# Attention and mixture-of-experts kernel: both heads of the 64-row query tile on one set of partitions

## The chip, the cores and the metric

The kernel runs on one core of a Trainium2 chip. The metric is the device time of one execution in microseconds (us). Engines go by the names of the profile: PE (matmul), PEld (its weight load), DVE, ACT, POOL, and SP, which issues most transfers.

## What is computed

The reference, cut to what matters (B, H, S, D = 4, 8, 576, 64; 512 columns in the model, 2048 in the hidden layer):

```python
scores = scale * np.matmul(q, k.transpose(0, 1, 3, 2))
a = np.exp(scores - scores.max(-1, keepdims=True))      # causal
a /= a.sum(-1, keepdims=True) + 1e-09
local = np.matmul(a, v)
phi = lambda x: np.where(x > 0, x, np.exp(x) - 1.0) + 1.0
mem_out = (phi(q) @ M_prev) / (phi(q) @ z_prev + 1e-6)
g = 1.0 / (1.0 + np.exp(-beta))
x = (g * mem_out + (1 - g) * local)                     # to [2304, 512]
r = np.maximum(x @ w_in, 0.0)
out = (s * (r * r) + b) @ w_out
```

## The kernel before, in words

There are three stages. The first runs from the start to about 271 us: the attention of 16 pairs of heads, four batches of four pairs, g = 0 to 15, with the first product (x @ w_in) of the batches that are done woven in. The second, to 357 us, is the rest of the first product, while `w_out` is converted (`conv64`). The third is the second product (`product`).

**A pair.** The two heads j = 0, 1 lie on partitions 0 to 63 and 64 to 127 of the operands of PE. The 576 query rows are cut into tiles i = 0 (64 rows) and 1 to 4 (128 rows each). `scores` (L357) works in three steps, named here Sg.0 (tiles 3 and 0), Sg.1 (tiles 2 and 1) and Sg.2 (tile 4, which takes both of the `sb` buffers). Pairs below 8 multiply in float32 (L370), the others ("fast") in three products of a float32r high and low part (L364), which `split` (L391) makes. For each tile and head `red` (L374, DVE) adds the mask and takes the smallest of each row, `ex` (L381, ACT) takes the exponential and its row sum, DVE sums and inverts (L440, L441), and `scale` (L386, POOL or DVE) scales. Tile 0 uses all 128 partitions for each head in this, with its 64 rows there twice. `phi` (L284) puts phi(q)/(phi(q)·z) of each tile beside it in `P` (`put`, L316). `bank` (L459) transposes `P` in four steps Tg.0 to Tg.3. Each of them reads two halves of the partitions, which go to two `tb` buffers: partitions 0 to 63 (half h0) and 64 to 127 (h1). The step Tg.3 holds the first-column blocks of tiles 0, 1 and 2, and tile 0 is read from h1 alone. `copy` (L472, ACT or DVE) takes the buffers to SBUF. `second` (L510, step Ag) multiplies by V and M, and L541 (ACT) and L542 (DVE) write x as a high and a low part, `xs`, with the first 64 rows apart in `x4`.

**The first product.** A group m (m0 to m40) is one block of 128 hidden columns of one batch (`first`, L596). Its PE work is two halves of six matmuls (`mm1`, L581), each half for two pairs. Its result is taken out of PSUM by a `Relu` on ACT (L609) and stored by SP (L610). `HOME` says whether it lies in a `tb` or an `sb` buffer; m40 lies in `sb`. The weights are converted in pieces (`convert`, L550); `HIGH` and `LOW` choose their engine. The second stage goes on with the same `mm1` into eight `hps` tiles, which take the PSUM of all `sb` and `tb` buffers over, the first that of the buffer sb0.

**What sets the order.** In the first stage each step carries the keys that it reads and writes, and a table of numbers, `ORDER`, says for each engine in which order its steps are issued; `Plan.deal` (L76) interleaves them, and puts warm-up matmuls (L247) into gaps of PE. Letters in `RELU`, `ZMUL`, `PUTS`, `COPY`, `SCAL` and `QL` choose the engine of a step for each pair. In the later stages a scheduler orders ACT and DVE.

```python
            for i, c0, n, o in group:                  # scores, L358
                if fast:                               # L359
                        if i == 0 and h == 0:          # bank, L465
                            continue
```

Of the kernel before, what the change touches and what calls it, by code (L numbers as in the profile page):

```python
# [141 lines left out]
def attention_moe_kernel(  # L142
# [187 lines left out]
    def attention(g):  # L330
# [78 lines left out]
        for v, group in enumerate(visits):  # L409
# [3 lines left out]
            if fast:  # L413
                cost = sum(n + 32 for _, _, n, _ in group) / 800 + 0.05
            add("PE", cost, lambda group=group, ps=ps: scores(group, ps), r,
                [(x, u, k) for x in ("qh", "ql") for k in range(2)] if fast else [("qk", u, k) for k in range((1, 2, 2, 3)[v] if g == 0 else 1)] + [("qk", 0, "d")] * (g == 0),
                [("sc", g, v), "visit"], take=[(ps, "S")] * (2 if v == len(visits) - 1 else 1), mode="row")
# [5 lines left out]
            tiles = [(i, o - c0) for i, c0, n, o in group if c0 + n == QW[i]]
            for k, (i, o) in enumerate(tiles):
                for j in range(2):
# [9 lines left out]
            keys = [("sm", u, i, j) for i in mine for j in range(2)]  # L435
            inv = [("sr", u, i, j) for i in mine for j in range(2)]
# [574 lines left out]
```

## Time and profile before

| | |
|---|---|
| runs | 540.35, 540.95 and 540.98 us, median 540.95 us |
| the profiled execution | 540.74 us |
| its span, first to last instruction | 538.9 us (1.84 us lie around it) |
| granted clock of TensorE | 1.00 throughout |
| busy | PE 529.4, DVE 406.8, ACT 408.1, POOL 276.4 us |
| moved by transfers | 81.51 MB |

The busy times are to be read by stage. In the second and third stage the order of PE hardly leaves a gap, and in the first stage the stretch up to some 56 us, before the first group m0, is another case than what follows it.

### The profile page before, as it was taken

The page shows a single profiled execution, that of the slowest core. Times are in us where ns is not written, and L with a number is a line of the kernel's source. Part 1 is how long each engine was busy: PE and PEld are TensorE (multiplying, and loading weights), DVE is VectorE, ACT ScalarE, POOL GpSimd, SP SyncE. Part 2 cuts the span into 40 slices and gives each one's busy share as a digit, 9 for nine tenths or more (in the row PEclk, how much of TensorE's full clock was granted, in tenths as well). Part 3 has the DMA queues.
Part 4 walks back from the last instruction along what each step waited for, and adds up shares of the span by engine and source line. Part 5 has one row for each costly group of instructions (what it writes and reads, how often), then busy time and mean ns, then how long its engine had stood idle before and what let it go on. Part 6 is the DMA issues. An engine that isn't in the chain of part 4 may idle for free.

```text
span 538.9 us, 11602 instructions
## 1 busy us (share of the span) xinstructions
PE 529.4 (98%) x4158; PEld 444.4 (82%) x4158; DVE 406.8 (75%) x986; ACT 408.1 (76%) x898; POOL 276.4 (51%) x275
## 2 busy tenths in 40 slices
PE   8989999999999999999999999999999999999997
PEld 6767777777878778877788888899999998999996
DVE  5999998998877958334169796435798889889873
ACT  6999999889987637547346679769987887897840
POOL 4999557663784623022100001407768768768760
PEclk9999999999999999999999999999999999999999
DMA  7666667755243621121294746356354353452101
GB/s 223 183 178 193 227 219 253 227 155 196 89 150 101 223 84 59 61 79 44 90 376 165 267 174 219 128 192 204 110 161 121 115 167 114 129 174 89 40 30 40
DMA packets 56666, 81.51 MB, mean 151 GB/s; under 512 B 7584, under 2 KB 39072, under 8 KB 56608
## 3 DMA queue, kind: packets, MB, share of 16 engines
q1 hardware_dynamic: 54064, 78.63, 44.8%
q10 hardware_dynamic: 2544, 2.14, 1.2%
q8 instruction: 33, 0.54, 0.4%
q14 instruction: 25, 0.20, 0.1%
HBM read 57.15 MB, written 23.59 MB: 150 GB/s over the span
## 4 chain that ended last, share of the span: by engine, by line
PE 90%; ACT 6%; DVE 2%; issue 1%; DMA 1%; ACTq 0%; DVEq 0%
PE yps L866 12%; PE yps L870 11%; PE sb L520 7%; PE tb L586 7%; PE tb L587 6%; PE tb L588 6%; PE hps L586 5%; PE hps L587 5%; PE hps L588 5%; PE yps L869 5%; PE yps L868 5%; PE tb L468 4%; PE sb L364 4%; ACT P L383 3%; PE sb L370 2%; PE sb L586 1%
## 5 line engine op out<-in xcount | busy, mean ns | idle before, releaser
L389 POOL TENSOR_SCALAR P<-P,sr,omg 128x448 f32<-128x448 f32 (+4 forms) x120 | 89.2, 758 | 37.0 <-DVE sr L441 26.3
L870 PE MATMUL yps<-rb,op 128*128 128x256 f32 x360 | 101.1, 281 | 0.0
L383 ACT ACTIVATE P<-P,mn 128x448 f32<-128x448 f32 (+4 forms) x160 | 90.0, 568 | 9.6 <-DVE mn L377 9.3
L377 DVE CUSTOM_DVE_ANT_0 P<-sb,mask 128x320 f32<-128x320 f32 (+4 forms) x160 | 72.6, 480 | 24.4 <-PE sb L364 21.8
L866 PE MATMUL yps<-rb,op 128*128 128x512 f32 x216 | 76.9, 396 | 0.0
L870 PEld LDWEIGHTS yps<-rb,op 128*128 128x128 f32 x360 | 67.9, 189 | 0.0
L846 POOL TENSOR_TENSOR sum<-src 128x512 f32<-128x512 f32 x10 | 13.0, 1298 | 91.2 <-ACT src L830 76.6
L854 POOL TENSOR_TENSOR op<-src,op 128x512 fp32r<-128x512 f32 x30 | 43.9, 1484 | 20.2 <-ACT op L853 20.1
L877 DVE TENSOR_TENSOR yu<-yu,yps 128x256 f32<-128x256 f32 x90 | 36.5, 414 | 20.0 <-PE yps L870 19.0
L866 PEld LDWEIGHTS yps<-rb,op 128*128 128x128 f32 x216 | 40.6, 188 | 9.0
L468 PEld LDWEIGHTS tb<-ident,P 64*128 64x128 f32 x928 | 35.9, 139 | 9.6 <-issue 4.3
L468 PE MATMUL tb<-ident,P 64*128 64x64 f32 x928 | 40.9, 226 | 2.2 <-DVE xs L542 0.7
L868 PE MATMUL yps<-rb,op 128*128 128x256 f32 x144 | 40.5, 281 | 0.0
L869 PE MATMUL yps<-rb,op 128*128 128x256 f32 x144 | 40.5, 281 | 0.0
L853 ACT CAST op<-src 128x512 fp32r<-128x512 f32 x50 | 30.5, 615 | 12.0 <-PE yps L870 9.6
L854 DVE TENSOR_TENSOR op<-sum,op 128x512 fp32r<-128x512 f32 x36 | 38.7, 1075 | 0.3 <-ACT op L853 0.2
L593 ACT ACTIVATE r<-hps 128x256 f32<-128x256 f32 x62 | 21.8, 385 | 19.4 <-DMA r_d<-r 14.4
L854 POOL TENSOR_TENSOR op<-w1H,op 128x512 fp32r<-128x512 f32 x24 | 35.0, 1489 | 0.0
L318 POOL TENSOR_TENSOR P<-qs,nrm 128x384 f32<-128x384 f32 (+1 forms) x24 | 18.8, 797 | 31.5 <-DVE nrm L311 23.0
L586 PE MATMUL tb<-xs,w0H 128*128 128x512 f32 x80 | 32.9, 412 | 0.0
L383 ACT ACTIVATION_READ_ACCUMULATOR P<-P,mn 128x1 f32 x160 | 32.3, 202 | 0.0
L370 PE MATMUL sb<-qk 64*128 64x288 f32 (+4 forms) x192 | 30.3, 411 | 1.9 <-DVE mn L377 1.7
(177 smaller groups left out, 1618.5 us busy)
## 6 DMA issues: line engine op xcount, KB each, us to landing
r_d<-r SPq DMA_DIRECT2D x41, 256.0 KB, 2.3
src<-r_d SPq DMA_DIRECT2D x20, 512.0 KB, 4.4
qk<-in_qk_t_dram SPq DMA_DIRECT2D x15, 576.0 KB, 5.0
raw<-in_moe_w_out_dram SPq DMA_DIRECT2D x16, 512.0 KB, 6.2
w1H<-r_d SPq DMA_DIRECT2D x16, 512.0 KB, 4.7
xa<-in_moe_w_in_dram SPq DMA_DIRECT2D x12, 512.0 KB, 4.8
r_d<-r SPq DMA_DIRECT2D x48, 128.0 KB, 1.9
qs<-in_q_rows_dram SPq DMA_DIRECT2D x16, 320.0 KB, 3.2
```

Source lines behind the costliest of these rows:

```text
L377: nc.vector.tensor_tensor_reduce(P[:, j, PB[i] + 64:PB[i] + 64 + n], at(ps, j, o, n), m, -SCALE, 3.0e38, ALU.add, ALU.min, mn[:, j, i:i + 1])
L383: nc.scalar.activation(pt, pt, AF.Exp, scale=-1.0, bias=mn[:, j, i:i + 1], accum_out=sm[:, j, i, 0:1])
L389: e.tensor_scalar(pt, pt, sr[:, j, i:i + 1], omg[:, h:h + 1], ALU.mult, ALU.mult)
L468: nc.tensor.transpose(TB[ps[h]][:, o[h]:o[h] + 64], P[rs, j, c:c + 128], ident[rs, rs], tile_position=(64 * h, 0))
L586: nc.tensor.matmul(ps, lhsT=wH[:, p, fs], rhs=xs[:, 0], start=p == 0, stop=False)
L587: nc.tensor.matmul(ps, lhsT=wH[:, p, fs], rhs=xs[:, 1], start=False, stop=False)
L588: nc.tensor.matmul(ps, lhsT=wL[:, p, fs], rhs=xs[:, 0], start=False, stop=p == NP - 1)
L854: (nc.gpsimd if m in ONPOOL else nc.vector).tensor_sub(L, x, H.bitcast(F32))
L866: nc.tensor.matmul(tile, lhsT=H, rhs=B, start=f == 0, stop=False)
L868: nc.tensor.matmul(ps, lhsT=H, rhs=B[:, 0], start=f == 0, stop=False)
L869: nc.tensor.matmul(ps, lhsT=H, rhs=B[:, 1], start=False, stop=False)
L870: nc.tensor.matmul(ps, lhsT=L, rhs=B[:, 0], start=False, stop=f == KF - 1)
```

## The change

1. Tile 0: the rows of head j go to partitions 64j to 64j + 63 of one slot of `P`. `red` works on 64 partitions for each head. One exponential, sum, reciprocal and scale then serve both heads; the exponential waits for both reductions. The scale needs the gates of both heads in one column, `OM`, which POOL fills once at the start. `phi` still leaves phi of tile 0 in a slot of each head, and one added 64 x 64 multiplication writes head 1's on its partitions.
2. Tg.3 transposes tile 0 of head 0 from half h0 and that of head 1 from h1: five transposes in each half, where there were four and six. Its buffers are copied in two pieces each (256 and 64 columns), four copies where there were two.
3. Fast pairs: tile 0's scores are taken in float32 like those of the first eight pairs; the split of q leaves 128 columns out.
4. `EARLY` is 2: m0 and m1 are issued in quarters, one for each pair (six quarters behind A3, the first of both ahead of it).
5. All letters, `HOME` and `ORDER` are new.

```diff
-                if fast:
+                if fast and i:
...
         def red(i, j, o, ps):
             n = QW[i]
+            if i == 0:
+                rs = slice(64 * j, 64 * j + 64)
+                nc.vector.tensor_tensor_reduce(
+                    P[rs, 0, PB[0] + 64:PB[0] + 128], at(ps, j, o, n)[rs], mask[rs, 576:640], -SCALE, 3.0e38, ALU.add, ALU.min, mn[rs, 0, 0:1])
+                return
...
-            e.tensor_scalar(pt, pt, sr[:, j, i:i + 1], omg[:, h:h + 1], ALU.mult, ALU.mult)
+            e.tensor_scalar(pt, pt, sr[:, j, i:i + 1], omg[:, h:h + 1] if i else OM[:, p:p + 1], ALU.mult, ALU.mult)
...
-            for k, (a, z) in enumerate(((QF, QF + S), (0, QF))):
+            for k, (a, z) in enumerate(((QF, QF + S), (128, QF))):
...
-                    add("ACT", EXP[i], lambda i=i, j=j: ex(i, j), r + 0.15 + 0.01 * k, [("mn", u, i, j)],
-                        [("p", u, i, j), ("sm", u, i, j)])
+                    if i or j:
+                        add("ACT", EXP[i], lambda i=i, j=j * (i > 0): ex(i, j), r + 0.15 + 0.01 * k, [("mn", u, i, h) for h in ((j,) if i else range(2))],
+                            [("p", u, i, j), ("sm", u, i, j)] + [("p", u, 0, 0), ("sm", u, 0, 0)] * (i == 0))
...
-                        if i == 0 and h == 0:
+                        rs = slice(64 * h, 64 * h + 64)
+                        if i == 0:
+                            if h == j:
+                                nc.tensor.transpose(
+                                    TB[ps[h]][:, 0:64], P[rs, 0, c:c + 128], ident[rs, rs], tile_position=(64 * h, 0))
                             continue
...
-            elif h:
-                put(F[:, :, 0:384].rearrange("p j (r c) -> p j r c", c=128)[:, :, :, 0:64],
-                    t[:, 0:384].rearrange("p (j r c) -> p j r c", j=2, c=64))
             else:
-                put(half(F[:, :, 64:320]), t[:, 0:256].rearrange("p (j r c) -> p j r c", j=2, c=64))
+                put(half(F[:, :, 64:320]), t[:, 64:320].rearrange("p (j r c) -> p j r c", j=2, c=64))
+                put(F[:, h, 0:64], t[:, 0:64])
...
+        if EARLY:
+            for p in range(NP):
+                add("PE", cost / 2, lambda p=p: mm1(part(), b, f, p, 1), 1000 + m - NP + p,
...
-    HIGH, LOW = "PPAPAAPPAAAAAAAAAAPA", "PDPDDPPDDDPDPDDDDDDD"
+    HIGH, LOW = "AAPPAAPAAAAPAAAAAAPA", "PPPDDDPPDDDDDDDPDDDD"
...
-    EARLY = 1
+    EARLY = 2
```

The table's new order at the places of which the prediction speaks. First PE around A3, the pair that completes the first batch; L468 is T3.3, L370 S5.1, L520 A3 and L586 to L588 group m0. Before:

```order
L468 MATMUL tb_101<-ident,P_121 128x64
L370 MATMUL sb_97<-qk_107 128x320 x2
L370 MATMUL sb_97<-qk_107 128x192 x2
L520 MATMUL tb_99<-F_125,V_123 64x320 x2
L520 MATMUL tb_99<-pt,V_123 64x256 x2
L520 MATMUL tb_99<-F_125,V_123 64x128 x2
L520 MATMUL tb_98<-F_125,V_123 64x256 x2
L520 MATMUL tb_98<-pt,V_123 64x256 x6
L520 MATMUL tb_98<-F_125,V_123 64x128 x2
L586 MATMUL tb_100<-xs,w0H 128x512
L587 MATMUL tb_100<-xs,w0H 128x512
L588 MATMUL tb_100<-xs,w0L 128x512
```

And now, where L484 is T3.3, L534 is A3, and L600 to L602 are m0 (in tb_101) and m1 (in tb_98):

```order
L484 MATMUL tb_99<-ident,P_122 128x64
L600 MATMUL tb_101<-xs,w0H 128x512
L601 MATMUL tb_101<-xs,w0H 128x512
L602 MATMUL tb_101<-xs,w0L 128x512
L600 MATMUL tb_98<-xs,w0H 128x512
L601 MATMUL tb_98<-xs,w0H 128x512
L602 MATMUL tb_98<-xs,w0L 128x512
L534 MATMUL tb_99<-F_126,V_124 64x320 x2
L534 MATMUL tb_99<-pt,V_124 64x256 x2
L534 MATMUL tb_99<-F_126,V_124 64x128 x2
L534 MATMUL tb_100<-F_126,V_124 64x256 x2
L534 MATMUL tb_100<-pt,V_124 64x256 x6
```

S5.1 now lies ahead of T3.3, and the first quarters of m0 and m1 stand between T3.3 and A3.

Second, ACT at the end of the first stage. L479 copies a buffer of T15.1, L609 is a group's relu (r_127<-sb_96 that of m40), L541 writes the x of A15, L196 and L593 belong to the second stage. Before:

```order
L609 ACTIVATE r_128<-tb_100 128x512
L479 COPY F_125<-tb_100 128x2x4x64
L479 COPY F_125<-tb_101 128x2x4x64
L609 ACTIVATE r_127<-sb_96 128x512
L541 CAST x_137<-sb_97 128x64
L541 CAST xs<-sb_97 128x512
L196 ACTIVATE stg<-raw 128x512 x2
```

And now (L493 copies a buffer of T15.1, L555 writes x, L632 is the relu, L607 belongs to the second stage):

```order
L555 CAST x_138<-sb_97 128x64
L493 COPY pt<-tb_98 128x8x64
L493 COPY pt<-tb_100 128x8x64
L555 CAST x_138<-sb_97 128x64
L555 CAST xs<-sb_97 128x512
L632 ACTIVATE r_128<-sb_96 128x512
L607 ACTIVATE r<-hps 128x256 x2
```

The relu of m40, from sb_96, has moved behind both of A15's casts. On PE, A15 is followed in both kernels by the first matmul into `hps`, which takes that buffer.

Third, DVE at the same end, from the last pair's other tiles on. L377 is a reduction of `red` (128x576 that of S15.2), L389 a scale, L440 and L441 the sum and the inverse, L542 the low part of x for A14. Before:

```order
L389 TENSOR_SCALAR P_121<-P_121,sr_119,omg 128x64 x2
L377 ISA P_121,mn_115<-sb_97,mask 128x576
L377 ISA mn_115 128x1
L389 TENSOR_SCALAR P_121<-P_121,sr_119,omg 128x320 x2
L377 ISA P_121,mn_115<-sb_96,mask 128x576
L377 ISA mn_115 128x1
L440 TENSOR_REDUCE sr_119<-sm_117 128x2
L441 RECIPROCAL sr_119<-sr_119 128x2
L542 TENSOR_TENSOR x_137<-sb_96,x_137 128x64
```

And now (L495 copies a buffer of T14.2, L497 and L498 copy T15.3, L388 is the reduction, L453 and L454 sum and invert, L400 is the scale of tile 4; behind it come the two copies of T15.0 and then A14's low parts):

```order
L495 COPY F_125<-tb_100 128x2x4x64
L497 COPY F_126<-tb_99 128x2x2x64
L498 COPY F_126<-tb_99 128x64
L388 ISA P_122,mn_116<-sb_97,mask 128x576
L388 ISA mn_116 128x1
L388 ISA P_122,mn_116<-sb_96,mask 128x576
L388 ISA mn_116 128x1
L453 TENSOR_REDUCE sr_120<-sm_118 128x2
L454 RECIPROCAL sr_120<-sr_120 128x2
L497 COPY F_126<-tb_100 128x2x2x64
L498 COPY F_126<-tb_100 128x64
L400 TENSOR_SCALAR P_122<-P_122,sr_120,omg 128x576 x2
```

The scales of the last tile have come to DVE (POOL made them before), and its copies of T14.2, T15.3 and T15.0 stand around that tile's work. On PE, S15.2 has moved to a place behind T15.3, with T15.0, a half of m39, A14 and a half of m40 between it and T15.1.

## Rows read from the trace of the kernel before

**Rows 1.** By stretch: length, busy PE, PEld, DVE, ACT, POOL (instructions), clock, DMA share, GB/s.

```profile
16.30:56.60 40.30, 37.69 (x466) 27.56 (x462) 39.39 (x145) 40.30 (x122) 35.87 (x46) 1.00 0.63 196
56.60:110.00 53.40, 53.40 (x437) 40.76 (x436) 50.25 (x144) 50.69 (x131) 32.16 (x35) 1.00 0.67 216
...
215.00:271.00 56.00, 56.00 (x504) 43.00 (x502) 18.26 (x69) 29.03 (x77) 10.56 (x16) 1.00 0.21 74
271.00:357.00 86.00, 86.00 (x470) 74.86 (x469) 61.47 (x118) 58.60 (x129) 8.48 (x6) 1.00 0.60 212
```

**Rows 2.** Waits of PE, 0 to 271 us: total, times, longest.

```profile
PE tb L468 <- DVE nrm L311: 0.6, 1, 0.6
```

**Rows 3.** PE's groups by form, 56.6 to 271 us: busy time, mean of one.

```profile
L364 PE MATMUL sb<-qks 64*128 64x64 f32 x48 | 3.5, 244 | 0.0
...
L370 PE MATMUL sb<-qk 64*128 64x64 f32 x8 | 0.7, 244 | 0.0
```

**Rows 4.** Timeline of PE around T8.3: start, duration, line, count.

```profile
140.33 0.46 PE L468 MATMUL tb<-ident,P 64*128 64x64 f32 x8
140.61 0.38 PE L364 MATMUL sb<-qks 64*128 64x288 f32 x1
140.63 0.28 PE L468 MATMUL tb<-ident,P 64*128 64x64 f32 x2
140.73 0.38 PE L364 MATMUL sb<-qks 64*128 64x288 f32 x2
```

**Rows 5.** Timeline of PE, a run of groups from switch to switch: first matmuls of its halves.

```profile
259.25 0.50 PE L586 MATMUL sb<-xs,w0H 128*128 128x512 f32 x1
...
260.74 0.40 PE L586 MATMUL tb<-xs,w0H 128*128 128x512 f32 x1
...
263.48 0.39 PE L586 MATMUL sb<-xs,w1H 128*128 128x512 f32 x1
...
264.93 0.28 PE L468 MATMUL tb<-ident,P 64*128 64x64 f32 x2
```

**Rows 6.** Timeline of all engines around A3.

```profile
52.41 0.52 ACT L484 COPY F<-tb 128x256 f32<-128x256 f32 x1
...
52.67 0.63 ACT L481 COPY F<-tb 128x384 f32<-128x384 f32 x1
...
53.04 0.60 ACT L566 ACTIVATE xa<-xa 128x256 f32<-128x256 f32 x1
...
53.35 0.20 PEld L520 LDWEIGHTS tb<-F,V 128*64 128x64 f32 x4 [0.36 <-ACT F L481]
...
54.66 0.34 ACT L383 ACTIVATE P<-P,mn 128x64 f32<-128x64 f32 x1
...
54.99 0.66 ACT L383 ACTIVATE P<-P,mn 128x448 f32<-128x448 f32 x1
```

**Rows 7.** Timeline of ACT at the end of the first stage.

```profile
267.83 0.60 ACT L609 ACTIVATE r<-sb 128x512 f32<-128x512 f32 x1 [0.55 <-ACT F L479]
271.07 0.21 ACT L541 CAST x<-sb 128x64 fp32r<-128x64 f32 x1 [2.65 <-PE sb L520]
271.18 0.59 ACT L541 CAST xs<-sb 128x512 fp32r<-128x512 f32 x1
```

**Rows 8.** Timeline of PE at the same place.

```profile
267.67 0.76 PE L520 MATMUL sb<-F,V 128*64 128x320 f32 x4
...
270.96 0.50 PE L586 MATMUL hps<-xs,w1H 128*128 128x512 f32 x1
```

**Rows 9.** Groups by form, whole span, ACT and DVE: busy time, mean of one.

```profile
L383 ACT ACTIVATE P<-P,mn 128x576 f32<-128x576 f32 x32 | 25.1, 784 | 5.3 <-DVE mn L377 5.3
...
L377 DVE CUSTOM_DVE_ANT_0 P<-sb,mask 128x576 f32<-128x576 f32 x32 | 23.5, 750 | 10.5 <-PE sb L364 10.5
...
L477 DVE COPY pt<-tb 128x512 f32<-128x512 f32 x18 | 11.8, 676 | 7.1 <-PE tb L468 6.9 <-PE sb L520 0.2
...
L389 DVE TENSOR_SCALAR P<-P,sr,omg 128x576 f32<-128x576 f32 x10 | 6.5, 663 | 0.1
```

More of the change, by code (lines that the diff above doesn't have):

```diff
@@ L231, in attention_moe_kernel @@
     NRM = two([128, 5, 2, 1], "nrm")
+    OM = ap1.tile([128, NP], F32, name="om")
     MN, SM, SR = two([128, 2, 5], "mn"), two([128, 2, 5, 2], "sm"), two([128, 2, 5], "sr")
@@ L413, in attention @@
             if fast:
-                cost = sum(n + 32 for _, _, n, _ in group) / 800 + 0.05
+                cost = sum(max(107, (n + 32) / 2.4 + 2) for i, _, n, _ in group if i) * 0.003 + (0.22 if v == 0 else 0.05)
             add("PE", cost, lambda group=group, ps=ps: scores(group, ps), r,
-                [(x, u, k) for x in ("qh", "ql") for k in range(2)] if fast else [("qk", u, k) for k in range((1, 2, 2, 3)[v] if g == 0 else 1)] + [("qk", 0, "d")] * (g == 0),
+                [(x, u, k) for x in ("qh", "ql") for k in range(2)] + [("qk", u, 0)] * (v == 0) if fast else [("qk", u, k) for k in range((1, 2, 2, 3)[v] if g == 0 else 1)] + [("qk", 0, "d")] * (g == 0),
                 [("sc", g, v), "visit"], take=[(ps, "S")] * (2 if v == len(visits) - 1 else 1), mode="row")
@@ L422, in attention @@
                     take=[(free, "T")], give=[(free, 0, "T")], mode="row")
+            heads = lambda i: range(2) if i else range(1)
             tiles = [(i, o - c0) for i, c0, n, o in group if c0 + n == QW[i]]
@@ L434, in attention @@
                 continue
[L435 to L436 removed]
+            keys = [("sm", u, i, j) for i in mine for j in heads(i)]
+            inv = [("sr", u, i, j) for i in mine for j in heads(i)]
             low = sorted(mine)
@@ L442, in attention @@
             for k, i in enumerate(mine):
-                for j in range(2):
+                for j in heads(i):
                     if SCAL[g][i] == "D":
@@ L500, in attention @@
             for h in range(2):
-                cost = dict(A=0.48 if k < 3 else 0.26 + 0.11 * h, D=0.58 if k < 3 else 0.33 + 0.13 * h)
+                cost = dict(A=0.48 if k < 3 else 0.36, D=0.58 if k < 3 else 0.45)
                 c = COPY[g][k]
@@ L579, in convert, with mm1 @@
             add("POOL", 1.27, lambda: nc.gpsimd.tensor_sub(L, w, H.bitcast(F32)), rank, [B_, ("WH", n)], [("WL", n)], fixed=0.1)
-    def mm1(ps, b, f, half):
+    def mm1(ps, b, f, half, n=NP // 2):
         wH, wL = W[2 * f // NF]
         fs = slice(128 * f % (DFF // 2), 128 * f % (DFF // 2) + 128)
-        for p in range(NP // 2 * half, NP // 2 * half + NP // 2):
+        for p in range(n * half, n * half + n):
             xs = X4[:, p] if b == B else XS[(b * NP + p) % 8]
@@ L604, in first @@
         cost = 6 * (CM / 2400 + 0.0125)
-        add("PE", cost, lambda: mm1(part(), b, f, 0), 1000 + m, x(0) + w(0) + (x(1) + w(1)) * (not EARLY),
+        if EARLY:
+            for p in range(NP):
+                add("PE", cost / 2, lambda p=p: mm1(part(), b, f, p, 1), 1000 + m - NP + p,
+                    [("xs", (b * NP + p) % 8, c, q) for c in range(2) for q in range(2)] + [(k, KEY[f, p]) for k in ("WH", "WL")],
+                    [("h", m), "seq"], take=[(ps, pool)] * (p == 0), mode="full")
+                yield
+            add("ACT", 0.49, lambda: nc.scalar.activation(r, part(), AF.Relu), -1, [("h", m)], [("r", m % NR)], give=[(ps, 0, pool)])
+            add("SP", 0.4, lambda: nc.sync.dma_start(r_d[b][:, f], r), -1, [("r", m % NR)], ["st"], bytes=262144)
+            return
+        add("PE", cost, lambda: mm1(part(), b, f, 0), 1000 + m, x(0) + w(0) + x(1) + w(1),
             [("h", m), "seq"], take=[(ps, pool)], mode="full", slack=0.3)
@@ L658, in attention_moe_kernel @@
                 ahead = [first(m, *MM[m], True) for m in todo[:EARLY]]
-                for _ in range(2):
+                for _ in range(NP + 1):
                     for some in ahead:
```

31 lines of the change are left out of this document (19 added, 12 removed), and 99 rows, old and new, of the table ORDER.

## The prediction

> **What bounds the kernel now.** I read the busy times first: PE has 529.4 us of the span of 538.9, so time is won where PE works, or where it waits. The table by stretch tells the two apart [rows 1]. From 56.6 us on PE is busy in every microsecond of the rows shown, 53.40 of 53.40, 56.00 of 56.00 and 86.00 of 86.00: there only less work on PE, or a wait that the change brings, counts, and DVE (50.25 of 53.40) and ACT (50.69) are slack that PE does not ask for. From 16.3 to 56.6 us it is ACT that is full, 40.30 of 40.30, with DVE at 39.39 and PE at 37.69. This is the fill, which ends when A3 has run and the first product feeds PE. The granted clock is 1.00 in all these rows, the upper level of 2.4 GHz, and nothing here makes PE pause long, so no term is for the clock. The waits of PE show one of some size behind 56.6 us, 0.6 us for phi's norm [rows 2]. Last I read the seams: A3, and the step from A15 into the second stage.
>
> The sum is made against the profiled execution, 540.74 us; the median of the runs, 540.95, lies 0.21 above it. About 0.2%, 1.08 us, is what a measurement of this kernel can tell from no change: faster is below 539.87, slower above 542.03.
>
> **The change part by part.**
>
> *Tile 0's scores of the eight fast pairs.* All eight lie behind 56.6 us, on PE's path. The form now has 48 records with 3.5 us of busy time, 0.44 us for a pair's six; the float32 form of the same 64 columns has 8 records for two pairs with 0.7 us, 0.35 us for a pair's four [rows 3]. So 8 x 0.09 = **-0.7 us**. Bounds: 0, if what is saved is only the overlapping tail of a record; -1.2, if the time goes by records (two of six, 8 x 0.15). I take the rows' own ratio.
> The Trainium skill ("FP8 and Floating Point Precision", TensorE Precision Notes) says that true float32 takes four passes through the array, which speaks against this part: four passes against the three products of now would make it 8 x 0.15 = +1.2 us, by an estimate from that page. The rows just named disagree for this width, and I go by them.
>
> *Five transposes in each half instead of four and six.* Around T8.3 the first record of the next step starts at 140.61, on h0, ahead of the last two transposes of T8.3 at 140.63, which are h1's; h1's first of the next step follows at 140.73 [rows 4]. So the halves run each at its own pace and h1 is behind by two transposes, 0.12 us, 0.06 each. The longer half sets when a step over the whole array can begin: it loses one, 0.06 us, in each of the 12 pairs from g = 4 on. 12 x 0.06 = **-0.75 us**; bounds 0 (h1 is caught up anyway) and -1.0 (0.08 each).
>
> *Switches.* A run of group halves costs more at its ends: the first half after a switch took 1.49 us (259.25 to 260.74), the last 1.45 (263.48 to 264.93), those between 1.37 (260.74 to 263.48 for two) [rows 5]: 0.2 us a run. By the order of PE there were 31 runs and now 33, of which one is the pair of quarters ahead of A3, priced with the fill. One more run: **+0.2 us**.
>
> *The fill.* ACT, which is full here, loses an exponential of 64 columns with its readout for each pair, 0.33 us (54.66 to 54.99), and copies Tg.3 in 2 x 0.26 + 2 x 0.11 = 0.74 us instead of 0.26 + 0.37 = 0.63 (52.41, 52.67, 53.04 [rows 6], and 271.07 to 271.18 for 64 columns [rows 7]). That is -0.22 a pair, -1.1 for five. Of the first eight pieces of weights ACT now makes five high parts instead of three, at about 0.26 for 256 columns: +0.5. ACT is left with -0.6. On PE, A3 waited 0.36 us for the copy of T3.3 [rows 6]. S5.1 covered part of that copy; it now lies earlier, and two quarters, 1.37 us (half of two halves) and a switch, cover it instead. So A3 comes some 1.2 us later by this alone, and 1.37 us less follows it: -0.2. The -0.6 reaches A3 only where PE waits for ACT. I take **-0.5 us** together. The ends: -1.8, if A3 comes 0.6 earlier and all of the quarters fall into waits; +0.5, if the two high parts delay the weights and nothing else is won. What is late next is m2's weights: DVE, at 39.39 of 40.30, must end their low parts for m2 as early as m2 is brought forward.
>
> *Waits behind 56.6 us.* The new order moves all of them. The one of 0.6 us may go, or one like it come: **0**, with -0.6 and +0.6. The joint exponential waits for one reduction more, and the exponentials behind it on ACT wait with it; the slack of ACT hides this (without it, one reduction each time).
>
> *The seam into the second stage.* The first `hps` tile takes the buffer sb0, where m40 lies, and its first matmul waits for m40's relu. Before, this relu ran at 267.83, while A15 was on PE (267.67 to 270.96), and PE went on at 270.96 without a gap [rows 7, 8]. Now it stands on ACT behind the two casts of A15, which can't start before A15 ends. By the times of before: casts at 271.07 and 271.18, the second to 271.77, the relu from about 271.67 (neighbours on ACT overlap by 0.1), 0.60 long, to 272.3. PE stands from 270.96 to 272.3: **+1.35 us**, bounds +1.2 and +1.5. Nothing hides it, as the second stage has no gap on PE, 86.00 of 86.00 [rows 1], in which to win it back.
>
> *At nothing:* the added 64 x 64 multiplication of phi, and the 0.1 us more of copies where DVE makes them, lie in the slack of DVE and POOL behind 56.6 us; OM's two copies lie in the start, where POOL is not full. Without this cover each would cost a few tenths of a microsecond a pair. Four fewer scales and sums are off PE's path as well. The scheduler orders ACT and DVE differently in the second stage; their 58.60 and 61.47 us in 86 hide it [rows 1].
>
> Sum: -0.7 - 0.75 + 0.2 - 0.5 + 0 + 1.35 = -0.4, or 540.34 against 540.74; on the median's footing **540.5 us**. The saved work of PE is given back at the seam.
>
> **The rivals.**
>
> *The fill gives its far end.* For it: PE has 2.6 us of gaps there, and warm-up matmuls besides, ACT is full, and both parts of the change ease just that. Against it: DVE is as full as ACT, and gets little relief. Fill -1.8 instead of -0.5: 540.5 - 1.3 = 539.2.
>
> *Slower: DVE is late with the last tile.* S15.2 is now issued behind T15.3; between it and T15.1, which needs its result, PE has only T15.0, a half of m39, A14 and a half of m40: 0.5 + 1.5 + 3.3 + 1.5 = 6.8 us by [rows 5, 8]. The chain on DVE and ACT is two reductions (0.83 each with the readout), two exponentials (the second ends some 1.1 behind the second reduction), sum and inverse (0.3), T15.3's copies (0.6), two scales (2 x 0.66), and the two copies of T15.0 (2 x 0.68), whose buffers T15.1's step takes: 6.3 us [rows 9], no more room than half a microsecond. Ahead of it DVE has two copies of T14.2 and T15.3's first, 2.0 us, of which S15.2 itself covers 0.9; a relu of 0.6 may stand in front of ACT's exponentials [rows 7]: 8.0 us, 1.2 too late. If DVE is so full there, T15.3 waits for its 64-column scale too, the last of five in a row, by a wait of the size of [rows 2], 0.6. It decides from 6.8 us on, and adds to the seam: 540.5 + 1.8 = 542.3. Against it: DVE had 18.26 us of work in the last 56 [rows 1], and most of what stands ahead may be done before S15.2 comes.
>
> *Matmuls keep their order.* If h0 could not run ahead of h1, both forms of Tg.3 would take ten records in turn, and that term would be 0: 541.25. The rows show h0 ahead of h1 at 140.61 [rows 4]. The Trainium skill ("TensorE: Matmul & The Clock Gate", Part 3, The mechanism) calls matmuls strictly first in, first out, start and end; by that page this rival holds, while the records above are out of step.
>
> *The change doesn't do what it says.* The quarters stand ahead of A3 in the order, but if m2's weights come no sooner, PE waits there for what it won. The fill is then 0 to +0.5: 541.0 to 541.5.
>
> **How the numbers follow.** My forecast, with its own range of 539.9 to 542.0, gets 0.39; the far end of the fill 0.27; the late last tile 0.15; matmuls in order 0.06; weights late 0.10; float32 dearer by the page's rule (540.5 + 0.7 + 1.2 = 542.4) 0.03. Faster: 0.27 and 0.03 out of the forecast's lower edge, 0.30. Slower: 0.15 + 0.03 and 0.02 of its upper edge, 0.20. The same: 0.50. The range goes from 538.8, 0.4 beyond the far end of the fill, to 542.3, which holds the late tile.
>
> **What would show it.** Right: A15 is followed by about 1.3 us without a matmul, and the waits name the relu of m40 there; from one Tg.3 to the next step both halves change over within 0.1 us; 64-column scores of fast pairs take 0.35 us a pair; A3 starts about a microsecond later than 53.35 us, and m2 not later than before. Wrong: no gap behind A15 (then 539.2); a wait of T15.1 for a scale; a wait of m2 for weights; a gain in the second or third stage, where I expect none.

## The result, and the profile after

The change makes the kernel slower: 544.54 us (median of 544.49 to 544.61, four runs) against 540.65 (540.28 to 540.98), a ratio of 1.0072 [1.0055, 1.0090]. The profiled execution took 544.49 us, with a span of 542.7. The forecast was 540.5 us, and the time lies outside the range.

By stretch, with the columns of [rows 1], the changed kernel:

```profile
16.30:56.60 40.30, 36.72 (x433) 27.30 (x430) 39.77 (x148) 37.83 (x112) 32.25 (x44) 1.00 0.57 170
56.60:110.00 53.40, 52.40 (x444) 39.40 (x444) 51.63 (x144) 50.61 (x137) 33.72 (x36) 1.00 0.67 213
110.00:160.00 50.00, 49.12 (x453) 37.62 (x451) 44.15 (x137) 41.53 (x111) 30.90 (x34) 1.00 0.55 169
...
271.00:357.00 86.00, 84.70 (x476) 73.12 (x473) 59.61 (x116) 57.42 (x125) 8.42 (x6) 1.00 0.61 212
```

In the fill ACT has come down from 40.30 to 37.83 us, as intended, and DVE has gone up to 39.77 of 40.30. Behind 56.6 us PE is no longer busy throughout. Its waits over the whole span; first the one for reductions as it was before, which like its counterpart lies in the fill:

```profile
PE sb L370 <- DVE mn L377: 1.7, 5, 0.6
```

```profile
PE sb L376 <- DVE mn L388: 3.2, 6, 1.6
PE hps L600 <- ACT r L632: 1.3, 1, 1.3
PE tb L248 <- DVE omg L252: 1.1, 1, 1.1
PE sb L600 <- DVE mn L384: 0.8, 1, 0.8
```

The second line of the change is the seam. The timeline of ACT there, then that of PE (as [rows 7, 8]):

```profile
273.47 0.21 ACT L555 CAST x<-sb 128x64 fp32r<-128x64 f32 x1 [4.26 <-PE sb L534]
273.58 0.59 ACT L555 CAST xs<-sb 128x512 fp32r<-128x512 f32 x1
274.05 0.61 ACT L632 ACTIVATE r<-sb 128x512 f32<-128x512 f32 x1
```

```profile
273.03 0.39 PE L534 MATMUL sb<-F,V 128*64 128x128 f32 x4
274.72 0.50 PE L600 MATMUL hps<-xs,w1H 128*128 128x512 f32 x1 [1.30 <-ACT r L632]
```

Before, the last record of A15 began 0.32 us ahead of `hps` (270.96 in [rows 8]), and no gap lay between them:

```profile
270.64 0.39 PE L520 MATMUL sb<-F,V 128*64 128x128 f32 x4
```

With the same distance PE would have gone on at 273.35 here, so 1.37 us are lost.

The rest of the loss is found with one more stretch, from the first matmul of A3 to the place where PE could take up `hps`. Before (A3 at 53.36), then after (A3 at 57.46):

```profile
53.36:270.96 217.60, 216.71 (x1949) 168.17 (x1949) 157.08 (x482) 163.53 (x431) 102.93 (x119) 1.00 0.44 143
```

```profile
57.46:273.35 215.89, 214.01 (x1927) 164.97 (x1926) 163.39 (x502) 154.76 (x408) 102.69 (x117) 1.00 0.44 140
```

The quarters ahead of A3, 1.60 us (55.86 to 57.46), have left this stretch, so the whole sum reads:

| term | predicted | measured |
|---|---|---|
| A3, less the quarters: 57.46 - 1.60 - 53.36 | -0.5 | +2.50 |
| PE's work behind A3: 214.01 + 1.60 - 216.71 | -1.25 | -1.10 |
| PE's gaps behind A3: 1.88 - 0.89 | 0 | +0.99 |
| the seam | +1.35 | +1.37 |
| first `hps`: 274.72 - 270.96 | -0.4 | +3.76 |

That is the whole difference of the profiled executions, 544.49 - 540.74 = 3.75. Work and seam came near the forecast; the fill and the gaps didn't.

### The profile page after: what moved, and what is told of

Its sections match the earlier page's. It is cut to its first block, busy times and chain, and to the rows that moved or that the text cites. A ratio compares the mean times of both kernels' runs of the same rounds, so it can differ in the third digit from the quotient of the medians.

```text
span 542.7 us, 11568 instructions
## 1 busy us (share of the span) xinstructions
PE 530.5 (98%) x4142; PEld 443.4 (82%) x4142; DVE 413.6 (76%) x1015; ACT 400.8 (74%) x875; POOL 273.8 (50%) x271
## 4 chain that ended last, share of the span: by engine, by line
PE 84%; DVE 11%; ACT 1%; issue 1%; DMA 1%; POOL 1%; ACTq 0%; DVEq 0%
PE yps L894 12%; PE yps L898 11%; PE sb L534 6%; PE hps L600 5%; PE hps L601 5%; PE hps L602 5%; PE yps L897 5%; PE yps L896 5%; PE tb L600 4%; PE tb L484 4%; PE tb L601 4%; PE tb L602 4%; DVE P L388 4%; PE sb L370 3%; PE sb L376 3%; PE sb L600 2%
## 5 line engine op out<-in xcount | busy, mean ns | idle before, releaser
L394 ACT ACTIVATE P<-P,mn 128x448 f32<-128x448 f32 (+4 forms) x144 | 84.2, 590 | 16.1 <-DVE mn L388 12.6
L400 POOL TENSOR_SCALAR P<-P,sr,omg 128x192 f32<-128x192 f32 (+3 forms) x90 | 69.9, 787 | 33.9 <-DVE sr L454 24.3
L388 DVE CUSTOM_DVE_ANT_0 P<-sb,mask 128x320 f32<-128x320 f32 (+3 forms) x128 | 67.2, 548 | 11.2 <-PE sb L370 10.3
L484 PEld LDWEIGHTS tb<-ident,P 64*128 64x128 f32 x896 | 34.6, 139 | 8.1 <-issue 3.5
L484 PE MATMUL tb<-ident,P 64*128 64x64 f32 x896 | 39.7, 226 | 1.4 <-ACT P L394 0.6
L376 PE MATMUL sb<-qk 64*128 64x64 f32 (+4 forms) x224 | 34.0, 399 | 3.5 <-DVE mn L388 3.2
L882 DVE TENSOR_TENSOR op<-sum,op 128x512 fp32r<-128x512 f32 x36 | 36.6, 1019 | 0.3 <-ACT op L881 0.2
L607 ACT ACTIVATE r<-hps 128x256 f32<-128x256 f32 x62 | 21.7, 382 | 15.4 <-DMA r_d<-r 9.3
L376 PEld LDWEIGHTS sb<-qk 64*128 64x128 f32 x224 | 21.6, 194 | 11.9 <-DVE mn L388 5.7
L881 ACT CAST op<-sum 128x512 fp32r<-128x512 f32 x36 | 22.3, 618 | 11.8 <-PE yps L898 10.1
L306 POOL TENSOR_TENSOR phr<-qs,z 128x640 f32<-128x640 f32 x11 | 18.4, 1674 | 24.9 <-DVE qs L302 16.1
```

Source lines behind the costliest of these rows:

```text
L376: nc.tensor.matmul(at(ps, j, o, n), lhsT=qk[rs, 128 * i:128 * i + 128], rhs=qk[rs, S + 64 + c0:S + 64 + c0 + n], start=True, stop=True, ti ...
L388: nc.vector.tensor_tensor_reduce(P[:, j, PB[i] + 64:PB[i] + 64 + n], at(ps, j, o, n), m, -SCALE, 3.0e38, ALU.add, ALU.min, mn[:, j, i:i + 1])
L394: nc.scalar.activation(pt, pt, AF.Exp, scale=-1.0, bias=mn[:, j, i:i + 1], accum_out=sm[:, j, i, 0:1])
L400: e.tensor_scalar(pt, pt, sr[:, j, i:i + 1], omg[:, h:h + 1] if i else OM[:, p:p + 1], ALU.mult, ALU.mult)
L484: nc.tensor.transpose(TB[ps[h]][:, o[h]:o[h] + 64], P[rs, j, c:c + 128], ident[rs, rs], tile_position=(64 * h, 0))
L881: nc.scalar.copy(H, x)
```

## The experiments

The kernel before took 540.4 to 540.5 us on these chips; ratios are to it. "A3" is the start of A3, "behind A3" the time from there to the first `hps`, "gaps" what of that PE was not busy, all from the profiled execution. In the change, `f_relu`, `k_swap` and `g_act` the quarters ahead of A3 put 1.60 us of work before A3 that elsewhere lies behind it. A3 also moves with the start, which differs between executions (last section): S1.0, the first scores of the second pair, begins at 11.03 us before and at 11.05 to 12.57 elsewhere.

| kernel | time, us | ratio | A3 | behind A3 | gaps |
|---|---|---|---|---|---|
| before | 540.4 | 1 | 53.36 | 217.60 | 0.89 |
| after | 544.54 | 1.0072 | 57.46 | 217.26 | 1.88 and the seam |
| `b_fp32` | 539.28 | 0.9980 [0.9971, 0.9989] | 54.02 | 215.53 | 0 |
| `c_bank3` | 540.83 | 1.0014 [1.0005, 1.0022] | 54.51 | 216.38 | 0.18 |
| `h_late` | 539.41 | 0.9976 [0.9965, 0.9986] | 54.61 | 215.10 | 0.18 |
| `m_late` | 540.51 | 0.9999 [0.9990, 1.0008] | 54.90 | 216.35 | 1.27 |
| `d_merge32` | 545.00 | 1.0083 [1.0070, 1.0096] | 58.41 | 216.71 | 1.65 |
| `f_relu` | 544.27 | 1.0068 [1.0056, 1.0080] | 58.01 | 215.93 | 1.95 |
| `k_swap` | 543.26 | 1.0058 [1.0041, 1.0075] | 56.78 | 215.86 | 1.86 |
| `l_late` | 544.54 | 1.0083 [1.0067, 1.0098] | 56.98 | 217.34 | |
| `g_act` | 546.85 | 1.0112 [1.0098, 1.0126] | 57.75 | 219.34 | |
| `x_dve` | 545.36 | 1.0087 [1.0071, 1.0103] | 57.61 | 217.49 | 0.65 |
| `x_dve1` | 541.75 | 1.0041 [1.0022, 1.0060] | 58.01 | 216.57 | |
| `x_dve_rest` | 543.23 | 1.0052 [1.0039, 1.0065] | 55.91 | 217.45 | |
| `x_act2` | 543.32 | 1.0052 [1.0039, 1.0064] | 56.71 | 216.75 | |
| `x_act` | 552.97 | 1.0226 [1.0210, 1.0242] | 62.94 | 219.07 | |

### Part by part on the kernel before

**Part 3 alone** (`b_fp32`), with the key that the multiplication now reads, and two loads of `qk` moved behind steps that still read it:

```diff
-                if fast:
+                if fast and i:
```

> The kernel before with part 3 alone (tile 0's scores of the eight fast pairs in float32; two loads of q and k move behind the scores that still read their buffer). Theory 1 (the parts save what I priced, the new order loses it): 0.7 us less than before, about 539.95 us, ratio 0.9987. Theory 2 (the parts themselves cost): by the four passes of float32, 1.2 us more, about 541.85 us. If the time went by records, 539.45 us.

It gains 1.1 us, and PE's work behind A3 falls by 216.71 - 215.53 = 1.18. Its later A3 is the start alone: from S1.0 to A3 it takes 42.32 us, before 42.33. **Part 2 alone** (`c_bank3`), 5 and 5 transposes, four copies:

```diff
-            o = [0, 0]
+            o = [64, 64] if k == 3 else [0, 0]
...
+                        if i == 0:
+                            if h == j:
+                                nc.tensor.transpose(
+                                    TB[ps[h]][:, 0:64], P[rs, j, c:c + 128], ident[rs, rs], tile_position=(64 * h, 0))
+                            continue
```

> The kernel before with part 2 alone (five transposes in each half of Tg.3, four copies instead of two; the softmax of tile 0 as it was). Theory 1: 12 x 0.06 = 0.75 us less, about 539.9 us. Theory 2: no gain on PE (matmuls in order, or the halves catch up anyway), and in the fill 0.1 us more of copies for each of five pairs: 540.65 to 541.2 us.

Behind A3 the work falls by 0.51, but A3 comes 1.15 us later, and not by the start (S1.0 is at 11.05): in its trace, part 2 costs in the fill what the transposes win behind it. **Parts 1 to 3** with the order, the letters, `HOME` and `EARLY` of before (`d_merge32`):

> Parts 1 to 3 of the change on the order, the letters and the single early group of the kernel before (steps that are gone leave their place empty). Theory 1: 0.7 + 0.75 us less on PE, and up to 0.6 less in the fill: 538.6 to 539.2 us; so the 3.9 us lost by the whole change belong to parts 4 and 5, the quarters and the order. Theory 2: the joint exponential, the added multiplication and the four copies delay the fill in any order: over 541.7 us.

This is as slow as the whole change. So a loss of this size needs neither the new order nor the seam: A3 comes 5.05 us late, and behind it work falls by 1.65 (216.71 to 215.06), near the two parts together, while the gaps rise to 1.65. It is not the same loss, though: in the fill the change loses 2.50, half of this, and its four runs have a mean granted clock of 1.000, where the four of `d_merge32` have 0.993 to 0.997. In the traces a mean below 0.998 goes with a stretch at 0.50 in the fill, 1.000 with none.

**The seam mended** (`f_relu`): the change, with m40's relu issued ahead of A15's casts.

```diff
+    some = 1132, 1403, 1405
+    for n, k in zip(some, sorted(ORDER[n] for n in some)):
+        ORDER[n] = k
```

> The changed kernel with the relu of m40 ahead of A15's two casts on ACT, nothing else. Theory 1: the gap of 1.3 us behind A15 goes, and all of it is won, as PE is full behind it: 544.5 - 1.35 = 543.15 us. Rival: the casts, now later, hold up the second stage and the time stays at 544.5 us.

On ACT, and on PE:

```profile
270.81 0.60 ACT L632 ACTIVATE r<-sb 128x512 f32<-128x512 f32 x1 [1.01 <-issue]
274.05 0.21 ACT L555 CAST x<-sb 128x64 fp32r<-128x64 f32 x1 [2.65 <-PE sb L534]
```

```profile
273.62 0.39 PE L534 MATMUL sb<-F,V 128*64 128x128 f32 x4
273.93 0.50 PE L600 MATMUL hps<-xs,w1H 128*128 128x512 f32 x1
```

The gap is gone, and the time behind A3 is 1.33 us shorter (217.26 to 215.93). The median falls by only 0.27: in the profiled execution PE's clock fell to 0.50 from 32.2 to 35.6 us, and A0 to A1 took 13.32 us instead of 12.40. All five runs have a mean clock of 0.996 or 0.997, so what the seam gave back was lost in the fill in each of them. The edit acts at 270 us; why the clock fell in this kernel's fill and not in the change's stays open. Without a fall one would expect 544.54 - 1.37 = 543.2 us, by an estimate.

### What fills the fill

The theory by then was that one of the change's small additions delays the fill. The change makes the 64 x 64 multiplication on DVE for the pairs 0 and 1 and on POOL for 2 to 4. `x_dve` adds to the kernel before this multiplication alone, on DVE for all of the pairs 0 to 4, into a buffer that nobody reads; `x_dve1` for pair 1 only, and `x_dve_rest` for 0, 2, 3 and 4.

```diff
+            if g < 5:
+                nc.vector.tensor_mul(SCR[64:128, 0:64], q[64:128, 0, 1], n[64:128, 0, 1].to_broadcast([64, 64]))
```

> The kernel before, and in each of the first five pairs one more 64 x 64 multiplication on DVE (phi of tile 0 for head 1, as the change adds it), into a buffer that nobody reads. Theory 3 (the fill is bound by DVE, whose idle time there is 1.1 us in 43; what is added to it, and what of it POOL then holds up, delays A3): five times 0.22 us and up to one collision of 1.2 us: A3 1 to 2.4 us later than 53.4, 541.4 to 542.8 us. My prediction's reading (ACT is full, DVE has room for it): no change, 540.4 us.

> The kernel before with the one added 64 x 64 multiplication on DVE in pair 1 alone. Theory 4 (this one runs into a scale of POOL, which held it 1.2 us in the run with five of them; DVE is late for PE, PE pauses, and its clock falls for 3.4 us): most of the 4.9 us of that run, 543 to 545 us, with A1 2 to 3 us later than 32.96 and the clock at the lower level for a while between 30 and 36 us. Rival (DVE's work adds up, pair by pair): a fifth, 541.4 us.

> The kernel before with the added multiplication on DVE in pairs 0, 2, 3 and 4, not in pair 1. Theory 4: four times 0.2 us and little more, 540.9 to 542 us, A1 at most 0.7 later, no fall of the clock. Rival (DVE's work adds up): four fifths of 4.9, 544.4 us.

Five instructions, of 0.22 us where nothing holds them (pair 0 of the change), cost 4.9 us; the expectation was far too low. A fall of the clock is part of it: the four runs have a mean of 0.994 to 0.997. Pair 1 shows how. Timeline of DVE, POOL and PE there, before:

```profile
26.97 0.58 DVE L318 TENSOR_TENSOR P<-qs,nrm 128x256 f32<-128x256 f32 x1
...
27.24 1.71 POOL L305 TENSOR_TENSOR phr<-qs,z 128x640 f32<-128x640 f32 x1
27.47 0.41 DVE L542 TENSOR_TENSOR xs<-tb,xs 128x256 fp32r<-128x256 f32 x1
...
28.95 1.31 PE L468 MATMUL tb<-ident,P 64*128 64x64 f32 x31 [0.74 <-DVE xs L542]
...
30.04 1.19 PE L370 MATMUL sb<-qk 64*128 64x448 f32 x8
```

With the multiplication (L326) of `x_dve1`:

```profile
27.65 0.59 DVE L319 TENSOR_TENSOR P<-qs,nrm 128x256 f32<-128x256 f32 x1
...
27.93 1.70 POOL L306 TENSOR_TENSOR phr<-qs,z 128x640 f32<-128x640 f32 x1
...
28.25 1.47 DVE L326 TENSOR_TENSOR r<-qs,nrm 64x64 f32<-64x64 f32 x1
...
29.75 0.42 DVE L548 TENSOR_TENSOR xs<-tb,xs 128x256 fp32r<-128x256 f32 x1
...
30.23 0.36 PE L474 MATMUL tb<-ident,P 64*128 64x64 f32 x1 [1.74 <-DVE xs L548]
...
31.24 1.97 PE L474 MATMUL tb<-ident,P 64*128 64x64 f32 x31 [0.65 <-DVE xs L548]
```

The multiplication takes 1.47 us and ends at 29.72, just behind POOL's multiplication with z (29.63; no scale, as the expectation had it), which runs beside it; the subtraction behind it, which reads `tb` in PSUM, ran through beside the same POOL instruction before (27.47). The subtraction frees the `tb` buffers that T1 writes, and is 2.3 us later (29.75 for 27.47), 0.7 of it by a later start (A0 at 22.72 for 22.03). So PE stands 1.74 and 0.65 us, where it stood 0.74 before. Then its clock falls. By stretch in `x_dve1`:

```profile
25.00:30.00 5.00, 3.46 (x36) 2.29 (x32) 4.71 (x13) 5.00 (x20) 5.00 (x7) 1.00 0.23 69
30.00:36.85 6.85, 5.98 (x57) 5.18 (x58) 5.19 (x19) 5.09 (x14) 3.88 (x8) 0.50 0.64 185
36.85:45.00 8.15, 7.32 (x83) 4.98 (x81) 8.11 (x31) 6.81 (x23) 6.81 (x10) 1.00 0.51 147
```

Between 30.00 and 36.85 us the granted clock is 0.50, the lower level of 1.2 GHz, and 57 matmuls stand where 83 did before in a stretch of the same length. This execution took 544.45 us. The nine runs are of two sorts, and their mean clock parts them: five took 541.5 to 541.75 us at 0.999 or 1.000, four 543.2 to 545.6 at 0.993 to 0.996. So the held multiplication costs some 1.2 us without a fall of the clock (541.65 against 540.40), 2.8 to 5.2 with one, and the expected 543 to 545 us came only with it. `d_merge32` meets the same: its multiplication of pair 1 took 1.44 us beside POOL's of 1.70. In the change, whose order is another, it took 0.73. The Trainium skill ("SBUF — State Buffer", Who interferes with whom) says that a DVE instruction with two inputs in SBUF and a GpSimd instruction that reads SBUF share a port, and that the second waits for the whole of the first. The rows agree: 1.47 us for the one with two SBUF inputs, 0.41 for the one that reads PSUM.

That is not the whole loss. `x_dve_rest` lost 2.8 us where at most 1.6 was expected, with A3 2.55 later (0.66 of it the start), A1 to A2 at 12.19 for 10.65, and no fall of the clock. In that stage PE waits 1.6 us for reductions of DVE, where it waited 0.3 before. The multiplication of pair 2 takes 0.52 us on DVE, and behind it a weight step comes just after a POOL step has begun:

```profile
42.48 0.73 POOL L585 TENSOR_TENSOR w0L<-xa,w0H 128x256 fp32r<-128x256 f32 x1
42.52 0.97 DVE L574 SCALAR_TENSOR_TENSOR xa<-xa 128x256 uint32<-128x256 uint32 x1
```

Before, this step came ahead of POOL's and took 0.41. `c_bank3` loses its time in the same stage (A1 to A2 at 12.05) and in the same way, without any multiplication:

```profile
41.31 0.73 POOL L580 TENSOR_TENSOR w0L<-xa,w0H 128x256 fp32r<-128x256 f32 x1
41.37 0.96 DVE L569 SCALAR_TENSOR_TENSOR xa<-xa 128x256 uint32<-128x256 uint32 x1
```

So a few tenths of a microsecond on DVE cost more than themselves, by what they make later steps run into.

**Is it DVE alone?** `x_act` and `x_act2` add five exponentials of 64 columns with their readout on ACT instead:

```diff
+            if g < 5 and i == 0 and j:
+                nc.scalar.activation(SCR[:, 0:64], mask[:, 0:64], AF.Exp, scale=-1.0, bias=mn[:, j, i:i + 1], accum_out=SCR[:, 64:65])
```

> The kernel before, and in each of the first five pairs one more exponential of 64 columns with its readout on ACT, into a buffer that nobody reads. My prediction's reading (ACT, 40.30 of 40.30, sets the fill's pace): five times 0.33 us, A3 1.65 us later, 542.1 us. Theory 3 (DVE sets it, and ACT's busy time is of records that lie over one another): 540.4 to 540.8 us.

> As the run with the added exponential on ACT, now reading the mask, which is there from the start (the first form read q and k, and waited 2.6 us for their next load, so that it told nothing of ACT). If ACT sets the pace of the fill as my prediction had it (no pause from 11 to 53 us): five times 0.33, A3 1.65 us later, 542.0 us, more if PE pauses and its clock falls. If DVE alone sets it: 540.4 to 540.8 us.

`x_act` is no evidence: it read `qk` instead of `mask`, and waited for the next load of it (ACT's timeline):

```profile
23.26 0.35 ACT L387 ACTIVATE r<-qk,mn 128x64 f32<-128x64 f32 x1 [2.58 <-DMA qk<-in_qk_t_dram]
```

`x_act2` loses 2.9 us, against 5 x 0.33 = 1.65 of added time on ACT (in its trace the next record starts 0.33 us behind an added one, 20.10 to 20.43). So ACT paces the fill as well. Its trace, too, has the clock at 0.50, from 32.3 to 35.7 us; but the one run of five with a mean of 1.000 took 543.24 us, so the loss beyond 1.65 is not the clock's alone, and stays open. Work added on either engine delays the fill; so relief of one need not show while the other gets more.

### Can the change be mended?

**The multiplication on ACT** (`g_act`, on `f_relu`):

```diff
-            vec.tensor_mul(o, q[64:128, 0, 1], n[64:128, 0, 1].to_broadcast([64, 64]))
+            nc.scalar.activation(o, q[64:128, 0, 1], AF.Copy, scale=n[64:128, 0, 1])
```

> The changed kernel with the relu of m40 ahead of A15's casts, and the added 64 x 64 multiplication of every pair on ACT instead of DVE or POOL. Theory 3: DVE is relieved of 0.22 us for each of pairs 0 and 1 and of the collision of 0.5 us at 26 us; A3 0.7 to 1 us earlier than with the relu alone, 543.2 to 543.6 us. Rival (the multiplication doesn't matter, the delay is the order's): 544.3 us as with the relu alone.

A0 to A1 fell to 11.40 us, but the next pairs gave it back. Behind A3 PE now waits for ACT's copies (from its waits there):

```profile
PE tb L484 <- ACT F L495: 1.1, 2, 0.8
```

But this is the smaller part of the 3.4 us by which its time behind A3 exceeds that of `f_relu`; most is longer busy time of PE (216.67 for 213.94 us), which is not explained. It is the slowest version but `x_act`. **One weight step on DVE later** (`k_swap`, on `f_relu`). The reason is in the change's timeline, DVE and POOL:

```profile
29.64 1.54 POOL L306 TENSOR_TENSOR phr<-qs,z 128x640 f32<-128x640 f32 x1 [1.62 <-DVE qs L302]
...
29.81 1.65 DVE L584 SCALAR_TENSOR_TENSOR xa<-xa 128x256 uint32<-128x256 uint32 x1
```

This step, some 0.42 us elsewhere, is held in the same way, and PE's next scores wait 1.64 us behind it.

```diff
+    for some in ((1132, 1403, 1405), (78, 184, 205, 185, 80, 207, 87)):
```

> The changed kernel with the relu of m40 ahead of A15's casts, and on DVE one step of the conversion of weights (at 29.81 us in the changed kernel, where POOL's product with z held it for 1.2 us) moved behind six steps, past two reductions that read PSUM. Theory 4: DVE wins the 1.2 us, A1 comes 1.2 us earlier and the time is 543.0 us. Rival (ACT, without a pause from A1 to A3, gives it back): 543.9 to 544.3 us.

The scores S3.0 come 2.1 us earlier (30.28 for 32.39), A1 only 0.13 sooner after A0 (12.27 for 12.40 in the change): the next wait takes the place of this one. The median is 1.0 us below that of `f_relu`, but its six runs have a mean clock of 0.999 or 1.000, so this may be the missing fall alone: the estimate for `f_relu` without one was 543.2.

**The first quarters behind A3 again** (`l_late`, on `f_relu`, ranks of 299, 425 and 426 exchanged):

> The changed kernel with the relu of m40 ahead of A15's casts, and the first quarters of m0 and m1 behind A3 instead of ahead of it (a switch less). If the quarters cover the copies of T3.3, as I priced them: A3 1.2 us earlier, 1.4 us more behind it: 544.4 us against 544.27. If they delay A3 for nothing: 543.0 us. If the copies then make A3 wait: 545.0 us.

Its median is 0.27 above that of `f_relu`, but three of its six runs have no fall of the clock and all of `f_relu` have one. Like with like, 545.0 to 546.6 us stand against 543.7 to 544.5 with a fall, and 543.9 to 544.1 against the estimated 543.2 without. So the quarters ahead of A3 win some 0.8 us. In its trace A3 waits 0.35 us for a copy again, as in [rows 6], and A3 comes only 0.5 us sooner (56.98 for 57.46) though 1.60 us of quarters no longer stand ahead of it.

**The parts only where the fill is over.** `h_late` is `b_fp32` with part 2 for the pairs from 4 on; `m_late` has part 3, and parts 1 and 2 for the pairs from 5 on, with the order of before.

```diff
+            o = [64, 64] if k == 3 and g > 3 else [0, 0]
```

```diff
+    LATE1 = 5
...
+            if i == 0 and g >= LATE1:
```

> The kernel before with part 3 (float32 scores of tile 0 in the fast pairs), and part 2 (five transposes in each half, four copies) for pairs 4 to 15 alone, behind the fill. Theory 3 (part 2 saves 1.2 us from A3 on, as its own run's trace has it, and loses the same in the fill): 539.28 - 0.7 to - 1.2 = 538.1 to 538.6 us. Rival (the two parts save the same waits): 539.3 us.

> Parts 1 to 3 of the change for pairs 5 to 15 alone, on the order, the letters and the single early group of the kernel before; pairs 0 to 4 as before. Theory 5 (the parts lose only in the fill, where the added work of DVE delays A3 by 4 to 5 us, and save about 1 us behind it): A3 at 53.4 to 54 us as before, 538.6 to 539.8 us. Rival (the joint softmax costs behind the fill too): 541 us and more.

Without the fill `m_late` loses nothing against before (its later A3 is the start: from S1.0 to A3 both take 42.33 us), so the loss of `d_merge32` is that of the first five pairs. But it wins nothing either: its work behind A3 is 215.08 us, that of `h_late` 214.92, and its gaps are 1.27 instead of 0.18 (0.89 before). These 1.1 us are about the distance of the two medians. So by these traces the joint softmax of tile 0 brings waits and no gain even behind the fill; which of its waits (two reductions ahead of one exponential, or the multiplication) is to blame was not taken apart. `h_late` and `b_fp32`, which can't be told apart, are the best versions found, 0.2% below the kernel before.

## Why the prediction was wrong

**Failed: "At nothing: the added 64 x 64 multiplication of phi, and the 0.1 us more of copies where DVE makes them, lie in the slack of DVE and POOL behind 56.6 us".** That cover was read behind 56.6 us, where eleven pairs lie. The first five lie in the fill, where my own table had DVE at 39.39 of 40.30 [rows 1]; there the multiplication, on DVE for all five, cost 4.9 us with falls of the clock in it (`x_dve`), in four pairs 2.8 without (`x_dve_rest`), and part 2 put A3 1.15 later (`c_bank3`). In the change DVE makes it in two pairs only, so these are no measure of its share there. I had written what it would cost without the cover, "a few tenths of a microsecond a pair", and not asked where the cover was missing.

**Failed: the fill at -0.5, with +0.5 as the far end.** Measured: +2.50. Only ACT's work was summed, not what parts 1 and 2 add on DVE. By groups, 11 us to A3 on DVE, before (L570 is a step on the weights, L481 and L484 the copies of Tg.3), then after (L584, L497 and L498, and the multiplication L326):

```profile
L570 DVE SCALAR_TENSOR_TENSOR xa<-xa 128x256 uint32<-128x256 uint32 x7 | 3.0, 431 | 0.0
...
L481 DVE COPY F<-tb 128x384 f32<-128x384 f32 x2 | 1.0, 518 | 0.0
...
L484 DVE COPY F<-tb 128x256 f32<-128x256 f32 x2 | 0.8, 414 | 0.0
```

```profile
L584 DVE SCALAR_TENSOR_TENSOR xa<-xa 128x256 uint32<-128x256 uint32 x7 | 4.1, 592 | 0.0
...
L497 DVE COPY F<-tb 128x256 f32<-128x256 f32 x4 | 1.7, 413 | 0.0
...
L326 DVE TENSOR_TENSOR P<-qs,nrm 64x64 f32<-64x64 f32 x2 | 1.0, 478 | 0.1
...
L498 DVE COPY F<-tb 128x64 f32<-128x64 f32 x4 | 0.8, 210 | 0.0
```

These groups grew by 2.8 us by their records: 1.1 by the held weight step, 1.0 by the multiplication, 0.7 by the copies. ACT's relief of 2.5 us could not show. From A0 to A1 ACT was busy throughout before; in the change it has 2 us to spare, and DVE is full (columns of [rows 1]):

```profile
22.03:32.96 10.93, 9.60 (x116) 6.98 (x115) 10.60 (x41) 10.93 (x34) 10.68 (x15) 1.00 0.42 116
```

```profile
23.46:35.86 12.40, 9.98 (x116) 6.69 (x115) 12.28 (x46) 10.36 (x30) 9.14 (x13) 1.00 0.43 128
```

Of the +2.50, 1.47 lie in this stage. 0.73 were there by S1.0 (11.76 for 11.03), by a start that differs between executions (last section), so that may not belong to the change; 0.70 came from S1.0 to A0, 0.14 from A1 to A2, and A2 to A3, less the quarters, gave 0.54 back. No run took the added DVE work out of the change's own first five pairs, so for the change DVE's part is read from its trace, not shown by a run.

**Held for the change, not for its neighbours: "nothing here makes PE pause long, so no term is for the clock".** The change's four runs read 1.000, so its loss is not the clock's. But the traces of `f_relu`, `d_merge32`, `x_dve`, `x_dve1` and `x_act2` have a fall, in `x_dve1` of 6.9 us at 0.50, behind pauses of PE near 30 us, and the runs of `x_dve1` put 1.5 to 4 us on it.

**Failed by its bounds: "Waits behind 56.6 us", 0 and at most +0.6.** The gaps grew by 0.99. The largest is at 99.49, on DVE and PE:

```profile
98.76 0.43 DVE L581 TENSOR_SCALAR xa<-xa 128x512 uint32<-128x512 uint32 x1 [0.27 <-ACT xa L580]
...
99.20 0.23 DVE L384 CUSTOM_DVE_ANT_0 P<-sb,mask 64x64 f32<-64x64 f32 x1
...
99.49 0.50 PE L600 MATMUL sb<-xs,w1H 128*128 128x512 f32 x1 [0.85 <-DVE mn L384]
```

The reduction of head 1 stands behind a weight step, and a group takes the buffer that it reads.

**Right: the seam**, +1.35 for 1.37, with the relu named; `f_relu` takes back 1.33.

**Right in kind: PE's work.** Part 3 gave -1.18 (`b_fp32`), the bound by records and not the -0.7 by the rows' ratio. In the change's profile, 56.6 to 273 us:

```profile
L376 PE MATMUL sb<-qk 64*128 64x64 f32 x40 | 3.3, 244 | 0.0
```

That is 0.33 us for a pair's four, against 0.44 before. The four passes that the prediction took from the Trainium skill ("FP8 and Floating Point Precision", TensorE Precision Notes) would have made this part dearer, 1.2 us by its estimate; it got cheaper. Part 2 gave -0.51 (`c_bank3`) and -0.61 (`h_late` against `b_fp32`: 214.92 for 215.53) instead of -0.75; a gain at all speaks for the halves running each at its own pace, against the rival of matmuls in order. Switches and order took back more than the 0.2: the change has 0.55 more than `d_merge32` (215.61 for 215.06).

**The rivals.** The slower one was another mechanism, DVE late with the last tile; no wait at T15.1 shows. Nor does one of m2 for weights: behind A3 PE's waits are for a reduction, an exponential and a copy. The fill's far end failed for the reason that I gave against it: DVE got no relief. The quarters ahead of A3, priced with the fill at -0.2, win more, some 0.8 (`l_late`).

## What to carry to other kernels

A kernel has stretches with different limits, and "off the critical path" must be asked for each of them: price an added instruction in every stretch where it is issued, and count each near-full engine there, letters and copies included, not only the one at 100%. Where two engines are both full, relief of one need not show; and a part that takes work off PE behind the fill can still win nothing when it is made there alone (`m_late`, `h_late`). Before a small DVE instruction is called 0.2 us, look at what POOL runs at that moment, and at which buffers are freed by what stands behind it. And where runs of one kernel differ, compare those of like granted clock.

## What was not expected of the hardware

- A DVE multiplication of 64 x 64, 0.22 us alone, took 1.47 us beside a POOL multiplication of 1.70, while a DVE subtraction with one input in PSUM kept its 0.41 beside the same.
- The same kernel's fill differs between executions. The twelve first score matmuls, in the timelines of before and then of after, at a granted clock that reads 1.00 in both:

```profile
4.60 1.38 PE L370 MATMUL sb<-qk 64*128 64x64 f32 x12 [0.25 <-DMA qk<-in_qk_t_dram]
```

```profile
4.61 2.51 PE L376 MATMUL sb<-qk 64*128 64x64 f32 x12 [0.21 <-DMA qk<-in_qk_t_dram]
```

They took 1.43 us in `f_relu`, whose program is the change's up to there, and 2.18 in `b_fp32`, which is the faster kernel: it does not go with the kernel. What sets it stays open.
- Pauses of PE of one to two microseconds in the fill were followed by 3.4 to 6.9 us at the lower clock in some traces (`x_dve1`, above) and by none in others (the change, after its 1.64 at 32.39). It differs between runs of one kernel too: four of nine of `x_dve1` and three of six of `l_late` have a mean clock below 0.998.
